# One weight job looked ahead instead of two, and h loaded straight into the place of its low part, in a fused attention and two-MoE kernel

## The chip, the cores and the metric

The kernel runs on one NeuronCore of a Trainium2 chip. The metric is the device time of one execution in microseconds (us). TensorE (PE in the profile) multiplies, VectorE (DVE), ScalarE (ACT) and GpSimd (POOL) do the work between, SyncE (SP) issues nearly all DMAs from one queue, in order. Each engine takes its instructions in program order, so one that waits holds up all that stand behind it on that engine.

## What is computed

```python
def _attn_ref(x, state):                       # x 8x8x512x64, state 8x8x32x64
    a = softmax(scale * x @ state.T)           # each token over the 32 states
    xread = a @ state
    a2 = softmax(scale * state @ x.T)          # each state over the 512 tokens
    sread = a2 @ x
    return concatenate([xread, sread], axis=2)

def _moe_ref(x, w_gate, w_val, w_out):         # 512 -> 1536 -> 512
    gate = 1.0 / (1.0 + np.exp(-(x @ w_gate)))
    return gate * (x @ w_val) @ w_out

def _moe2_ref(x, w_in, w_out):                 # 512 -> 2048 -> 512
    h = x @ w_in
    g = np.where(h >= 1, h, np.where(h <= -1, 0.0, (h + 1) ** 2 / 4))
    return g @ w_out
```

The attention's output, as 4352 tokens of 512 (8 batches of 512 tokens and 32 states), goes through the first MoE and then the second. All of it is float32. The kernel gets float32 accuracy by splitting every operand into a high part (rounded to the matmul's fp32r type) and a low part (what is left), and adding three products: high by high, high by low, low by high.

## The kernel before

The batches are handled in two groups of four. The stages that the change touches, in order of time, are the first gated pass (group 0, `gated(0)`), the first output pass (`output1(0)`, with the attention of group 1 worked in between as "items" of `slot1`), the second gated pass (`gated(1)`) and the second output pass (`output1(1)`). Then come the few tokens of the states, and the second MoE, which takes the second half of the time.

**A gated pass** makes h, the product of gate and value, without forming the attention's output. For every block of 64 rows of the weights a "pair" of matmuls on TensorE (L483) folds the state into them; ACT copies the result as the high half of a tile M (L488), and DVE takes the low half (L494). Then `quads` (L510) multiply M with the attention weights. Twenty-four steps i alternate gate (even, into PSUM set 0) and value (odd, into set 1). The sums of an even step are read by ACT's sigmoid (L551), those of an odd step by a product on DVE (L554); both are emitted in the next step, after its first three heads. A pair of step i goes to the other set: the pair of an odd step needs the set-0 sums of the step before to be read by the sigmoid.

**Weights** come as jobs through the class `Weights`. A job is loaded (tile `wraw`, three buffers, L146), ACT makes two words from it (`parts`: tiles `ca`, three buffers, L155, and `cy`, two buffers, L156), DVE joins them (`join`, L162 and L166), ACT takes the high part (`high`, L181, into the tile `w`), DVE or POOL the low part (`low`, L187). The tile `ca` is held from `parts` to `low`. One `slot` does one step of each, in the order `high`, `join`, `low`, `parts`, `load`; the list `mid` holds joined jobs that wait for `high`. `high` leaves a job alone while its kind is in `closed`; the kind "wo" (the weights of the first output pass) is closed until that pass begins, the kind "m1" (those of the second gated pass) until late in it. In the second gated pass there are two `w` tiles, and each is also stored to `ws_dram` (L466) before its buffer is used again.

**An output pass** multiplies h with w_out. It runs over 24 units (four batches b, six units m2 of 256 rows of h), each of four parts with six matmuls (L624 to L626; the first unit is taken in another order, L606). Before each part, `slot` works items or weight jobs. At unit i the kernel issues the load of unit i + 2 (`load_h`, tile `hraw`, two buffers, L584) and, in part 1, the split of unit i + 1 (`split_h`): ACT makes the high part `oh_hi` (L591), DVE the low part `oh_lo` (L593), two buffers each. After the sixth unit of a batch its sums, two PSUM tiles, are copied into tiles `ev1` by ACT (L632) and by DVE (L634) and stored (L635). In the first pass there is one `ev1` buffer, in the second two. The batches alternate between the PSUM sets; items use the set that the current batch leaves free, which is the set whose sums were just copied out.

Of the kernel before, what the change touches and what calls it, by code (L numbers as in the profile page):

```python
# [25 lines left out]
def attention_moe_moe_kernel(  # L26
# [104 lines left out]
    class Weights:  # L131
# [6 lines left out]
        def __init__(self):  # L138
            self.todo, self.loaded, self.first, self.mid, self.second = [], [], [], [], []

        def load(self, most=9):
            while self.todo and len(self.loaded) + len(self.first) < min(most, CB[0]):
                src, dst = self.todo.pop(0)
                r = conv.tile([128, 1024], U32, tag="wraw", name="wraw", bufs=CB[0])
                for o, i in src(r):
                    nc.sync.dma_start(out=o, in_=i.bitcast(U32))  # L146
                self.loaded.append((r, dst))
# [42 lines left out]

        def slot(self, low=None):
            self.high()
            if len(self.mid) < 2:
                self.join()
            self.low(low)
            if not self.first:
                self.parts()
            self.load()
            flush()
# [377 lines left out]
        return lambda r: [(r, w_out[128 * i : 128 * i + 128])], dst  # L577

    hr_t, h_t, acc_t = {}, {}, {}
    ev_bufs = 1  # L580

    def load_h(b, m2):
        t = hr.tile([128, 2, 512], F32, tag="hraw", name="hraw", bufs=2)
        nc.sync.dma_start(out=t, in_=h_dram[b // 4][:, 2 * m2 : 2 * m2 + 2, b % 4])  # L584
        hr_t[b, m2] = t

    def split_h(b, m2):
        t = hr_t.pop((b, m2))
        hi = hp_.tile([128, 2, 512], F32R, tag="oh_hi", name="oh_hi", bufs=2)
        lo = hp_.tile([128, 2, 512], F32R, tag="oh_lo", name="oh_lo", bufs=2)  # L590
        nc.scalar.activation(out=hi, in_=t, func=AF.Copy)  # L591
        h_t[1, b, m2] = (hi, lo)
        return lambda: nc.vector.tensor_tensor(  # L593
            out=lo, in0=t, in1=f32(hi), op=ALU.subtract
        )

    def out1_first(b, hi, lo, part):
# [16 lines left out]
    def out1(b, m, hi, lo, n, os):  # L614
# [11 lines left out]
            nc.tensor.matmul(out=ps, lhsT=wl[:, c], rhs=hi, start=False, stop=last)  # L626
        if m == NM1 - 1 and os[-1] == 3:
            for i in range(2):
                ev = hp_.tile([128, 2, 512], F32, tag="ev1", name="ev1", bufs=ev_bufs)
                evv = ev[:, :, :n]  # L630
                if i == 0:
                    nc.scalar.activation(out=evv, in_=acc[i][:, :, :n], func=AF.Copy)  # L632
                else:
                    nc.vector.tensor_copy(evv, acc[i][:, :, :n])  # L634
                nc.sync.dma_start(out=y_dram[b][:, 2 * i : 2 * i + 2], in_=evv)  # L635

    def output1(bg, slot):
# [5 lines left out]
        for i, (b, m2) in enumerate(us):  # L643
# [1 line left out]
                load_h(*us[i + 2])  # L645
            hi, lo = h_t.pop((1, b, m2))
            for part in range(4):
                low = split_h(*us[i + 1]) if part == 1 and i + 1 < len(us) else None
                slot(4 * i + part, 1 - b % 2)
                if low:  # L650
                    low()
                if i == 0:
                    if part < 3:
                        out1_first(b, hi, lo, part)
                    continue
                e = part // 2
                os = (0, 1) if part % 2 == 0 else (2, 3)
                out1(b, 2 * m2 + e, hi[:, e], lo[:, e], S, os)
# [373 lines left out]
    for w in PRE:  # L1032
# [45 lines left out]
    sgp = pool("sgp", side="right", stack=st_a)  # L1078
    hp_ = pool("hp", stack=st_h)
    weights.todo += [job_wo(k) for k in range(NM1)]  # L1080
    gated(
        0,
        q_ps,
        {14: lambda: load_h(0, 0), 18: lambda: load_h(0, 1), 23: lambda: split_h(0, 0)()},
    )


# [88 lines left out]


    closed.remove("wo")
    for hp in range(2):
        weights.high()  # L1180
        weights.low()
# [30 lines left out]

    hp_, ev_bufs = pool("hp1", side="right", stack=st_wo), 2
    wsp = pool("wsp", side="right", stack=st_wo)
    st_pa = ExitStack()
    pa = pool("pa", stack=st_pa)
# [131 lines left out]
```

## Time and profile before

| what | value |
|---|---|
| median of 3 runs | 1514.85 us (1513.44 to 1517.57) |
| the profiled execution: its own time | 1514.42 us |
| its span, first to last instruction | 1512.5 us |
| PE busy | 1452.5 us (96%) |
| DVE busy, ACT busy | 908.3 us (60%), 629.1 us (42%) |
| mean granted TensorE clock | 0.984 of full speed |
| first output pass, about 206 to 419 us | PE waits in it below |
| second gated pass, about 419 to 606 us | PE waits in it below |
| second output pass, about 606 to 737 us | PE never idle |

PE is busy nearly all the time, so the time can only fall where PE is idle or where it runs at the lower of its clock levels (0.50 in the rows), and it rises where a new wait reaches PE. In rows of the timeline the first number is the start in us from the span's start, the second the duration, and the bracket at the end tells how long the engine sat idle before the instruction and what ended that.

### The profile page before, as it was taken

The numbers are of one execution on the slowest core, as the hardware profiler recorded it, in microseconds if no ns is written. First come the engines' busy times: TensorE is split into PE (matmuls) and PEld (weight loads), VectorE is DVE, ScalarE is ACT, GpSimd is POOL, SyncE is SP. The second block draws the span as 40 slices with busy tenths as digits, with TensorE's granted clock in tenths as the row PEclk, the third lists the DMA queues.
The fourth block names the chain that finished last, engine by engine and source line by source line (L and its number), as shares of the span: only waits on it lengthen the run. The fifth ranks groups of instructions, "written<-read, shape, count | busy, mean of one in ns | idle before, by whom it ended". The sixth has DMA issues, their size and how long they took to land.

```text
span 1512.5 us, 28809 instructions
## 1 busy us (share of the span) xinstructions
PE 1452.5 (96%) x12176; PEld 1244.4 (82%) x12176; DVE 908.3 (60%) x1201; ACT 629.1 (42%) x896; POOL 32.0 (2%) x25
## 2 busy tenths in 40 slices
PE   7999989899969999999999999999999999999997
PEld 6677767787747778888998888888889899999997
DVE  6666656544346552444227675566655987777785
ACT  6655546343354542343126442233323544444342
POOL 2200003000000000000000000000000000000000
PEclk9999999999979999999999999999999999999999
DMA  6244557543545653675347873553334544344432
GB/s 214 79 156 169 194 177 250 170 158 108 186 168 196 225 209 113 210 248 196 140 171 247 269 247 139 195 182 136 128 140 143 179 140 134 125 134 140 140 126 84
DMA packets 143697, 255.63 MB, mean 169 GB/s; under 512 B 15056, under 2 KB 85712, under 8 KB 143568
## 3 DMA queue, kind: packets, MB, share of 16 engines
q1 hardware_dynamic: 143304, 253.54, 49.2%
q8 instruction: 95, 1.56, 0.4%
q10 hardware_dynamic: 264, 0.26, 0.1%
q14 instruction: 34, 0.28, 0.1%
HBM read 156.24 MB, written 97.52 MB: 168 GB/s over the span
## 4 chain that ended last, share of the span: by engine, by line
PE 84%; DVE 6%; ACT 3%; DMA 3%; issue 3%; SPq 1%; DVEq 0%; ACTq 0%
PE ps L510 15%; PE ps L216 9%; PE ps L218 9%; PE ps L217 9%; PE o L837 7%; PE o L839 7%; PE o L838 7%; PE ps L624 5%; PE ps L626 5%; PE ps L625 5%; PE ps L483 3%; DVE cy L162 1%; PE ps L293 1%; DVE hc L885 1%; ACT cy L156 1%
## 5 line engine op out<-in xcount | busy, mean ns | idle before, releaser
L510 PE MATMUL ps<-at_hi,M 32*128 32x512 f32 x3072 | 265.4, 404 | 9.2 <-DVE M L494 6.4
L839 PE MATMUL o<-w,hc 128*128 128x256 f32 x952 | 267.6, 281 | 3.3 <-DVE hc L885 3.3
L837 PE MATMUL o<-w,hc 128*128 128x256 f32 x952 | 267.4, 281 | 1.9 <-DVE sg L829 1.6
L838 PE MATMUL o<-w,hc 128*128 128x256 f32 x952 | 267.1, 281 | 0.0
L216 PE MATMUL ps<-y_hi,wi 128*128 128x512 f32 (+1 forms) x576 | 217.4, 377 | 0.0
L218 PE MATMUL ps<-y_hi,wi 128*128 128x512 f32 (+1 forms) x576 | 217.3, 377 | 0.0
L217 PE MATMUL ps<-y_lo,wi 128*128 128x512 f32 (+1 forms) x576 | 217.3, 377 | 0.0
L510 PEld LDWEIGHTS ps<-at_hi,M 32*128 32x128 f32 x3072 | 155.6, 187 | 56.7 <-issue 15.6
L839 PEld LDWEIGHTS o<-w,hc 128*128 128x128 f32 x952 | 180.7, 190 | 4.4 <-DVE hc L885 4.4
L837 PEld LDWEIGHTS o<-w,hc 128*128 128x128 f32 x952 | 181.5, 191 | 2.4 <-issue 2.2
L838 PEld LDWEIGHTS o<-w,hc 128*128 128x128 f32 x952 | 180.6, 190 | 0.0
L828 ACT ACTIVATE sg<-sg,half 128x1024 f32<-128x1024 f32 (+1 forms) x72 | 79.6, 1106 | 217.1 <-DVE sg L825 213.3
L510 PE MATMUL ps<-at_lo,M 32*128 32x512 f32 x1536 | 160.9, 398 | 0.0
L624 PE MATMUL ps<-oh_hi,wo 128*128 128x512 f32 x368 | 150.1, 408 | 3.0 <-ACT oh_hi L591 3.0
L625 PE MATMUL ps<-oh_lo,wo 128*128 128x512 f32 x368 | 145.7, 396 | 0.6 <-DVE oh_lo L593 0.5
L626 PE MATMUL ps<-oh_hi,wo 128*128 128x512 f32 x368 | 145.4, 395 | 0.0
L829 DVE TENSOR_TENSOR sg<-sg,ps 128x1024 f32<-128x1024 f32 (+1 forms) x72 | 83.7, 1162 | 86.7 <-ACT sg L828 86.7
L494 DVE TENSOR_TENSOR M<-ps,M 128x1024 fp32r<-128x1024 f32 x48 | 58.8, 1224 | 117.8 <-ACT M L488 117.8
L216 PEld LDWEIGHTS ps<-y_hi,wi 128*128 128x128 f32 x576 | 108.4, 188 | 20.2 <-ACT ev L632 0.2
L217 PEld LDWEIGHTS ps<-y_lo,wi 128*128 128x128 f32 x576 | 108.4, 188 | 20.0
L218 PEld LDWEIGHTS ps<-y_hi,wi 128*128 128x128 f32 x576 | 108.4, 188 | 19.8
L881 ACT ACTIVATE hc<-hc 128x512 fp32r<-128x512 f32 (+1 forms) x108 | 64.9, 602 | 124.1 <-DMA hc<-hd_dram 111.3
(120 smaller groups left out, 2132.7 us busy)
## 6 DMA issues: line engine op xcount, KB each, us to landing
hd_dram<-sg SPq DMA_DIRECT2D x64, 512.0 KB, 2.8
h_dram<-sg SPq DMA_DIRECT2D x48, 512.0 KB, 4.3
hraw<-h_dram SPq DMA_DIRECT2D x48, 512.0 KB, 4.8
hc<-hd_dram SPq DMA_DIRECT2D x96, 256.0 KB, 4.0
wraw<-in_moe_w_out_dram SPq DMA_DIRECT2D x28, 512.0 KB, 4.1
wraw<-in_moe_w_gate_dram SPq DMA_DIRECT2D x48, 256.0 KB, 2.9
wraw<-in_moe_w_val_dram SPq DMA_DIRECT2D x48, 256.0 KB, 3.3
ws_dram<-w SPq DMA_DIRECT2D x24, 512.0 KB, 5.1
```

What stands on the lines that cost most here:

```text
L216: nc.tensor.matmul(out=ps, lhsT=wh, rhs=vh, start=(i == 0), stop=False)
L217: nc.tensor.matmul(out=ps, lhsT=wh, rhs=vl, start=False, stop=False)
L218: nc.tensor.matmul(out=ps, lhsT=wl, rhs=vh, start=False, stop=(i == n - 1))
L510: nc.tensor.matmul(out=ps[r // 2][:, r % 2], lhsT=M[o, l, e, c], rhs=a[o, e], start=(h == 0 and j == 0), stop=(h == H - 1 and j == 2),)
L624: nc.tensor.matmul(out=ps, lhsT=wh[:, c], rhs=hi, start=first, stop=False)
L625: nc.tensor.matmul(out=ps, lhsT=wh[:, c], rhs=lo, start=False, stop=False)
L626: nc.tensor.matmul(out=ps, lhsT=wl[:, c], rhs=hi, start=False, stop=last)
L828: nc.scalar.activation(out=sg, in_=sg, func=AF.Square, bias=half, scale=0.5)
L829: nc.vector.tensor_tensor(out=sg, in0=sg, in1=ps, op=ALU.max)
L837: nc.tensor.matmul(out=ps, lhsT=wh, rhs=vh, start=start and i == 0, stop=False)
L838: nc.tensor.matmul(out=ps, lhsT=wh, rhs=vl, start=False, stop=False)
L839: nc.tensor.matmul(out=ps, lhsT=wl, rhs=vh, start=False, stop=last)
```

## The change

- `Weights` gets a number `ahead`, 1 at first: a slot joins a job only while fewer than `ahead` jobs stand in `mid` (2 before). It is set to 2 at step 18 of the first gated pass and back to 1 at the start of the first output pass.
- `load_h` writes h to the place where its low part will stand, three tiles `oh_lo0` to `oh_lo2` in turn, and the low part is taken in place. The tiles `hraw` are gone; two of the three new tiles take their room, so the total is the same and leaves room for a second `ev1` buffer in the first output pass.
- The split of unit 1 is emitted in part 0 of unit 0, ahead of that part's slot.

```diff
+            self.ahead = 1
...
         def slot(self, low=None):
             self.high()
-            if len(self.mid) < 2:
+            if len(self.mid) < self.ahead:
                 self.join()
...
     def load_h(b, m2):
-        t = hr.tile([128, 2, 512], F32, tag="hraw", name="hraw", bufs=2)
-        nc.sync.dma_start(out=t, in_=h_dram[b // 4][:, 2 * m2 : 2 * m2 + 2, b % 4])
+
+        k = m2 % 3
+        t = (hp_ if k == 2 else hr).tile(
+            [128, 2, 512], F32R, tag=f"oh_lo{k}", name=f"oh_lo{k}", bufs=1
+        )
+        nc.sync.dma_start(out=f32(t), in_=h_dram[b // 4][:, 2 * m2 : 2 * m2 + 2, b % 4])
         hr_t[b, m2] = t
...
     def split_h(b, m2):
-        t = hr_t.pop((b, m2))
+        lo = hr_t.pop((b, m2))
         hi = hp_.tile([128, 2, 512], F32R, tag="oh_hi", name="oh_hi", bufs=2)
-        lo = hp_.tile([128, 2, 512], F32R, tag="oh_lo", name="oh_lo", bufs=2)
-        nc.scalar.activation(out=hi, in_=t, func=AF.Copy)
+        nc.scalar.activation(out=hi, in_=f32(lo), func=AF.Copy)
         h_t[1, b, m2] = (hi, lo)
         return lambda: nc.vector.tensor_tensor(
-            out=lo, in0=t, in1=f32(hi), op=ALU.subtract
+            out=lo, in0=f32(lo), in1=f32(hi), op=ALU.subtract
         )
...
-                ev = hp_.tile([128, 2, 512], F32, tag="ev1", name="ev1", bufs=ev_bufs)
+                ev = hp_.tile([128, 2, 512], F32, tag="ev1", name="ev1", bufs=2)
...
-                low = split_h(*us[i + 1]) if part == 1 and i + 1 < len(us) else None
+                early = part == (1 if i else 0)
+                low = split_h(*us[i + 1]) if early and i + 1 < len(us) else None
...
+    def last_jobs():
+        weights.ahead = 2
+        load_h(0, 1)
+
     gated(
         0,
         q_ps,
-        {14: lambda: load_h(0, 0), 18: lambda: load_h(0, 1), 23: lambda: split_h(0, 0)()},
+        {14: lambda: load_h(0, 0), 18: last_jobs, 23: lambda: split_h(0, 0)()},
     )
...
     closed.remove("wo")
+    weights.ahead = 1
```

TensorE's and POOL's instructions stand in the same order as before, and through the first gated pass so do all others. Three places show what moves. The first is ACT at the start of the first output pass, before and then after (`e2` are the exponentials of the state's attention, `oh_hi` the high part of unit 1):

```order
L156 ACTIVATE cy_3527<-wraw_2870 128x512
L369 ACT_TABLE_LOAD
L369 ACTIVATE e2_283,r2_3504<-ps1_3492,m2_3501 128x512 x2
L369 ACTIVATE e2_355,r2_3521<-ps1_3509,m2_3518 128x512 x2
L155 ACTIVATE ca_3555<-wraw_2994 128x512
L156 ACTIVATE cy_3556<-wraw_2994 128x512
L591 ACTIVATE oh_hi_3571<-hraw_2874 128x1024
L181 ACTIVATE wo0_3_3583<-ca_3526 128x512
```

```order
L158 ACTIVATE cy_3526<-wraw_2870 128x512
L595 ACTIVATE oh_hi_3544<-oh_lo1_2874 128x1024
L371 ACT_TABLE_LOAD
L371 ACTIVATE e2_283,r2_3503<-ps1_3491,m2_3500 128x512 x2
L371 ACTIVATE e2_355,r2_3520<-ps1_3508,m2_3517 128x512 x2
L157 ACTIVATE ca_3556<-wraw_2994 128x512
L158 ACTIVATE cy_3557<-wraw_2994 128x512
L183 ACTIVATE wo0_3_3581<-ca_3525 128x512
```

The high part of unit 1 moves ahead of the table load and the four exponentials. On DVE the low part of unit 1 keeps its place, behind the sums of those exponentials.

The second place is ACT at the start of the second gated pass, with the semaphores that each instruction waits for, before and then after:

```order
L488 ACTIVATE M_5287<-ps0_5280 128x1024 [waits DVE_49,PE_49]
L181 ACTIVATE w_5290<-ca_3894 128x512 [waits DMAHW3_49]
L155 ACTIVATE ca_5295<-wraw_5044 128x512 [waits DMAHW2_49,DMAHW1_49,DVE_49]
L156 ACTIVATE cy_5296<-wraw_5044 128x512
L488 ACTIVATE M_5310<-ps1_5303 128x1024 [waits PE_49]
L181 ACTIVATE w_5313<-ca_5040 128x512 [waits DMAHW0_49]
L155 ACTIVATE ca_5318<-wraw_5125 128x512 [waits DMAHW7_49,DMAHW6_49,DVE_49]
```

```order
L490 ACTIVATE M_5254<-ps0_5247 128x1024 [waits DVE_49,PE_49]
L183 ACTIVATE w_5257<-ca_5010 128x512 [waits DMAHW1_49]
L157 ACTIVATE ca_5262<-wraw_5014 128x512 [waits DMAHW7_49,DMAHW0_49]
L158 ACTIVATE cy_5263<-wraw_5014 128x512
L490 ACTIVATE M_5277<-ps1_5270 128x1024 [waits PE_49]
L183 ACTIVATE w_5280<-ca_5090 128x512 [waits DMAHW6_49,DVE_49]
L157 ACTIVATE ca_5285<-wraw_5094 128x512 [waits DMAHW5_49,DMAHW4_49,DVE_49]
```

The kinds of instructions stay; the first `ca` no longer waits for DVE, and `w` now does. One job fewer is joined ahead during the first output pass (two DVE and two ACT instructions of it are gone there and come back near the end of the gated pass).

The third is SP in the first output pass, the loads of h (units 2 to 4) between the loads of w_out, before and then after:

```order
L584 DMA hraw_3543<-h_dram_0_99 128x2x512 [waits DMAHW2_49,Activation_49]
L146 DMA wraw_3559<-in_moe_w_out_dram 128x1024 [waits DMAHW3_49,DVE_49,Activation_49]
L146 DMA wraw_3593<-in_moe_w_out_dram 128x1024 [waits DMAHW4_49,DVE_49,Activation_49]
L584 DMA hraw_3603<-h_dram_0_99 128x2x512 [waits DMAHW5_49,Activation_49]
L146 DMA wraw_3615<-in_moe_w_out_dram 128x1024 [waits DMAHW6_49,DVE_49]
L146 DMA wraw_3643<-in_moe_w_out_dram 128x1024 [waits DMAHW3_49,DMAHW7_49,DVE_49,Activation_49]
L584 DMA hraw_3657<-h_dram_0_99 128x2x512 [waits DMAHW2_49,DMAHW0_49,Activation_49]
```

```order
L589 DMA oh_lo2_3542<-h_dram_0_99 128x2x512 [waits DMAHW2_49]
L148 DMA wraw_3560<-in_moe_w_out_dram 128x1024 [waits DMAHW3_49,DVE_49,Activation_49]
L148 DMA wraw_3591<-in_moe_w_out_dram 128x1024 [waits DMAHW4_49,DVE_49]
L589 DMA oh_lo0_3601<-h_dram_0_99 128x2x512 [waits DMAHW5_49,PE_49]
L148 DMA wraw_3613<-in_moe_w_out_dram 128x1024 [waits DMAHW6_49,DVE_49]
L148 DMA wraw_3640<-in_moe_w_out_dram 128x1024 [waits DMAHW3_49,DMAHW7_49,DVE_49,Activation_49]
L589 DMA oh_lo1_3654<-h_dram_0_99 128x2x512 [waits DMAHW0_49,PE_49]
```

The loads stand in the same places, but from unit 3 on they wait for PE: the tile that they fill was read by the matmuls of the unit three before.

## Rows read from the trace of the kernel before

**Rows 1.** Stretches: length, busy us of PE, PEld, DVE, ACT, POOL, clock, DMA.
```profile
425.00:610.00 185.00, 171.40 (x2447) 128.64 (x2440) 95.05 (x110) 82.96 (x109) 0.00 (x0) 0.94 0.50 184
...
423.81:450.74 26.93, 18.01 (x149) 11.12 (x149) 14.31 (x19) 14.19 (x21) 0.00 (x0) 0.69 0.60 209
450.74:456.90 6.16, 6.16 (x50) 4.53 (x54) 3.11 (x4) 2.63 (x4) 0.00 (x0) 0.51 0.10 16
...
610.00:740.00 130.00, 130.00 (x587) 108.06 (x587) 51.39 (x57) 43.76 (x57) 0.00 (x0) 1.00 0.59 196
```

**Rows 2.** Waits, 418 to 610 us: who waited for whom, total us, times, longest.
```profile
ACT ca L155 <- DVE w L187: 52.9, 19, 4.3
...
PE ps L483 <- ACT sg L551: 7.1, 8, 2.4
```

**Rows 3.** Timeline where the first batch of the first output pass ends.
```profile
264.31 8.71 SPq L635 DMA_DIRECT2D y_dram<-ev  x2
271.44 1.22 DVE L634 COPY ev<-ps 128x1024 f32<-128x1024 f32 x1 [7.67 <-DMA y_dram<-ev]
272.72 1.97 PE L386 MATMUL ps<-ident,e 128*128 128x128 f32 x8 [4.05 <-DVE ev L634]
...
277.38 1.10 PE L278 MATMUL ps<-ident,xa 128*128 128x128 f32 x8 [0.68 <-ACT e L317]
```

**Rows 4.** Timeline of the start of the first output pass.
```profile
219.84 0.17 DVE L377 TENSOR_SCALAR r<-r 128x2 f32<-128x2 f32 x1 [0.97 <-ACT e L369]
220.83 1.04 ACT L591 ACTIVATE oh_hi<-hraw 128x1024 fp32r<-128x1024 f32 x1
221.90 1.22 DVE L593 TENSOR_TENSOR oh_lo<-hraw,oh_hi 128x1024 fp32r<-128x1024 f32 x1 [0.38 <-ACT oh_hi L591]
221.92 0.79 PE L624 MATMUL ps<-oh_hi,wo 128*128 128x512 f32 x1 [2.96 <-ACT oh_hi L591]
223.18 0.80 PE L625 MATMUL ps<-oh_lo,wo 128*128 128x512 f32 x1 [0.46 <-DVE oh_lo L593]
```

**Rows 5.** Timeline of the start of the second gated pass.
```profile
419.85 1.02 ACT L488 ACTIVATE M<-ps 128x1024 fp32r<-128x1024 f32 x1 [1.27 <-PE ps L483]
...
421.40 1.23 DVE L634 COPY ev<-ps 128x1024 f32<-128x1024 f32 x1 [6.72 <-ACT w L181]
422.54 1.22 DVE L494 TENSOR_TENSOR M<-ps,M 128x1024 fp32r<-128x1024 f32 x1
...
423.81 0.79 PE L510 MATMUL ps<-at_hi,M 32*128 32x512 f32 x2 [2.38 <-DVE M L494]
...
425.00 0.69 DVE L187 TENSOR_TENSOR w<-ca,w 128x512 fp32r<-128x512 f32 x1
...
425.72 0.67 ACT L155 ACTIVATE ca<-wraw 128x512 f32<-128x512 f32 x1 [4.33 <-DVE w L187]
...
426.84 1.00 ACT L488 ACTIVATE M<-ps 128x1024 fp32r<-128x1024 f32 x1
...
443.92 1.23 DVE L494 TENSOR_TENSOR M<-ps,M 128x1024 fp32r<-128x1024 f32 x1 [2.19 <-ACT M L488]
...
447.11 0.68 ACT L155 ACTIVATE ca<-wraw 128x512 f32<-128x512 f32 x1 [2.70 <-DVE w L187]
...
450.74 1.65 PE L483 MATMUL ps<-w,sd 64*128 64x512 f32 x6 [2.44 <-ACT sg L551]
...
467.57 0.97 PE L483 MATMUL ps<-w,sd 64*128 64x512 f32 x6 [0.68 <-ACT sg L551]
```

**Rows 6.** DMAs issued 420 to 460 us: times issued, KB each, median us to landing.
```profile
ws_dram<-w SPq DMA_DIRECT2D x6, 512.0 KB, 3.7
```

**Rows 7.** Loads of h over both output passes: time to landing, 48 loads.
```profile
DMA to landing us min/median/max: 3.5/4.8/8.1
```

**Rows 8.** Timeline: TensorE's start and end of the second output pass.
```profile
606.05 0.50 PE L606 MATMUL ps<-oh_hi,wo 128*128 128x512 f32 x1
...
736.80 0.31 PE L216 MATMUL ps<-xs_hi,ws 128*128 128x256 f32 x1
```

## What the change will do to the time, forecast before it was run

> **What bounds the kernel now.** I read the page first: PE is busy 96% of the span, so a change that touches no matmul can only win where PE is idle or runs at its lower clock. Then the stretches, stage by stage [rows 1]. The second output pass shows PE busy 130.00 us of 130.00 at clock 1.00: nothing to win, only something to lose. The second gated pass shows 171.40 of 185.00 at a mean clock of 0.94. Its start is the weak place: of the 26.93 us from 423.81 to 450.74 PE works 18.01, much of it at the lower level, and the 6.16 us after that run at 0.51, the lower level of the two (1.2 GHz against 2.4). Then the waits of that pass [rows 2]: PE waits 7.1 us, eight times, for ACT's sigmoid, and ACT itself stands 52.9 us, 19 times, with the instruction that fills `ca` until DVE has taken the low part of a weight. Last the timeline at the three places where PE stands: the end of the first batch of the first output pass [rows 3], that pass's start [rows 4], the start of the second gated pass [rows 5].
>
> **One depth instead of two.** The 19 waits have a reason that can be counted in the code. `ca` has three buffers, each held from `parts` to `low`. Two jobs in `mid` and one between `high` and `low` fill them, so the `ca` of a slot needs the `low` of the same slot. That closes a ring over two engines, which [rows 5] shows: M's low part on DVE at 422.54, two joining instructions, `w` at 425.00 to 425.69 (3.15 us from 422.54), `ca` on ACT at 425.72, `cy`, and only then the next M, 1.12 us later at 426.84, 1.00 long, for which DVE waits. 3.15 + 0.03 + 1.12 + 1.00 + 0.04 = 5.34 us. The low part of M at 443.92 is four rounds later: 21.38 / 4 = 5.35. With one job in `mid` the third buffer was freed a slot earlier, and ACT fills it at once. What is late next: DVE's own four instructions, 3.15 us; ACT's own four, about 2.7 (M 1.00, `ca` and `cy` 1.12, `w` estimated at 0.6 from `ca`'s 0.67); and a new pair of waits, since `w` must now see the join of the slot before (over by then, as DVE joins ahead of its `low`), and each of the two `w` buffers must be stored before it is used again. Such a round, `low` 0.69, store landing 3.7 [rows 6], `w` about 0.6, is 5.0 us for two slots, though `w` stands behind M on ACT and can be pushed back by it. Bounds for a slot: 3.15 and, if the store always comes last behind M and the joins, about 4.3. I take 3.3, near DVE's, because the store's round is shorter than two of DVE's. Four rounds then take 13.2 us instead of 21.4: **8.2 us** less (4.2 to 8.8).
>
> From the last of these M to the pair at 450.74 lies a second part: ACT stands 2.70 us before `ca` at 447.11, then comes `cy`, the table load and the sigmoid that PE waits for. That wait goes too; the store may take some back. **2.0 us** (0.7 to 2.7). A check from PE's side: with 10.2 us gone, 16.7 of 26.93 remain for 18.01 us of matmuls, most of them at the lower level. So if PE stayed as slow as it is, it would be the bound, and 8.9 would be the gain; the shorter pauses should let some of it run at full speed. Afterwards 6.16 us run at 0.51, which costs 3.0; I take **1.0** of that back (0 to 3.0), as the pauses ahead are shorter but not gone.
>
> Later in the pass the same wait delays the sigmoid in each odd step: the first of the eight waits is the 2.44 at 450.74, the other seven sum to 4.7, each like the 0.68 at 467.57 [rows 2, 5]. ACT's wait before `ca` there is some 2.7 us (52.9 / 19), so the sigmoid can start when its sums are ready. **4.7 us** (3.5 to 4.7). The join that is no longer made ahead adds four instructions, 0.7 us each, near the end of the pass, where DVE and ACT are half busy (95.05 and 82.96 of 185.00): nothing. In the first gated pass the limit stops no job that moves, nothing.
>
> **Two `ev1` buffers in the first output pass.** DVE's copy of the first batch's second half stood 7.67 us until 271.44 for the store of the first half to leave the one buffer [rows 3]. Without that it runs 263.77 to 264.99; PE, free at 268.67, then finds its PSUM tile empty and saves 4.05. The eight transposes behind the pause took 1.97 against 1.10 for eight at full speed, and some matmuls behind them were slow too; together I add 1.5. **5.6 us** (4.05 to 6). Next late is the 0.68 before L278, which stays. The same happens to the last batch: the copy at 421.40 is put down to ACT's `w`, but it is the store issued when the first half was copied. M's low part can follow ACT's M, which ends at 420.87, instead of starting at 422.54: **1.65 us** [rows 5], and the matmuls at 423.81 come that much earlier. At the other two batches PE showed no such wait: nothing.
>
> **The early split of unit 1.** PE stood 2.96 us for the high part of unit 1 [rows 4]. That part now comes ahead of the exponentials, so the first matmul can go. But the second matmul wants the low part, and on DVE that stands behind the sums of those exponentials (the wait at 219.84), which the moved instruction pushes back by its 1.04, less the overlap of neighbours, 0.95. DVE had 0.38 to spare before the low part, so it comes 0.57 later, and PE with it. I expect no gain but a **loss of 0.55 us** (a gain of at most 0.5, a loss of 1.0); PE's wait is renamed.
>
> **Loads of h into the low part's place.** The load of unit i + 2 used to wait for the split of unit i, now for PE to finish unit i - 1, which is the start of unit i. A unit takes (736.80 - 606.05) / 24 = 5.45 us [rows 8]. From there to the start of unit i + 2 are 10.9 us; less the high part 1.04, the low part 1.22 and some 0.4 of hand-overs, a load may take 8.2. Loads took 3.5 to 8.1, 4.8 in the middle [rows 7]. So the cover is just enough, by the unit of matmuls between; if it fails, PE pays what is over 8.2. Behind the waiting load on SP stand the weights, the x tiles and the stores of the unit; the stores wait for PE at the end of a batch anyway, and the weights of this stage are wanted a slot or more later. **Loss 0.3 us** (0 to 3), from 0 because most loads are far from the edge.
>
> **Sum.** Against the profiled execution's own 1514.42 (span 1512.5): 8.2 + 2.0 + 1.0 + 4.7 + 5.6 + 1.65 - 0.55 - 0.3 = 22.3, so 1492.1. The median of the runs is 0.43 above the profiled one: 1492.5. The ends of the terms together give 1489 to 1501, but not all fall on one side.
>
> **Rivals.** (1) *The store's round takes the ring's place.* For it: DMA is busy 0.60 in the start of the gated pass [rows 1], and a faster chain asks more of it per us. Slots of 4.3: the four rounds give 4.2, the tail 0.7, the clock nothing: 22.3 - 4.0 - 1.3 - 1.0 = 16.0, 1498.5. (2) *The wait for DVE is only a name.* If DVE's and PE's order hold the slot at 5.34 whatever ACT does, only the `ev1` terms stay: 5.6 + 1.65 - 0.85 = 6.4, 1508. Against it: after each of these waits ACT goes on without a pause into the M that DVE waits for. (3) *Slower: loads come late.* The place is every unit from the third on, 22 in each output pass; the price is what a landing takes beyond 8.2 us. To eat the forecast it needs 0.5 us in each of 44 units, to end 4.5 us slower 0.61, so landings of 8.8 throughout; at 9.0 it would be 1492.5 + 35 = 1528. Against it: the longest of 48 took 8.1 [rows 7]. The Trainium skill (Trainium Kernel Development and Optimization, Best Practices) asks to double-buffer so that DMA overlaps compute, and a change that shortens both look-aheads goes against that; by that rule it would end here. The 52.9 us of ACT [rows 2] speak against the rule: there the second job in front is what makes an engine stand. (4) *The gains and costs cancel, or the change does not do what it says.* The order of the instructions shows the `ca` without DVE's wait, so this is small.
>
> **How the numbers follow.** The forecast, 1487 to 1496.5, has a chance of 0.68; (1), 1496.5 to 1502, 0.17; (2), 1503 to 1510, 0.07; (3) 0.04; (4) 0.04. The forecast and (1) hold 0.85, so the range is 1487 to 1502. About 0.3%, 4.5 us, is what a measurement of this kernel can tell from no change: faster by more 0.92, within it 0.04, slower 0.04.
>
> **What would show it.** ACT's wait for DVE before `ca` should be nearly gone in the second gated pass, the low parts of M 3.2 to 3.6 us apart at its start, and the 7.1 us of PE's waits for the sigmoid below 2. DVE's copy should follow ACT's within 3 us at the end of the first batch. PE should still stand 2.5 to 4.5 us at the start of the first output pass, now for the low part. In the second output pass PE should stay busy throughout. I am wrong if the M's stay 5.3 apart (2), if `w` waits for its store (1), or if PE waits for `oh_hi` in the output passes (3).

## The result, and the profile after

The changed kernel takes 1491.55 us (median of 4 runs, 1490.81 to 1496.89); the kernel before took 1515.78 beside it (4 runs, 1513.44 to 1517.57). The ratio is 0.985, with a 95% interval of 0.982 to 0.988: 1.5%, or 23 us between the means (24 between the medians). The forecast was 1492.5, from 1487 to 1502. The profiled execution took 1490.97 us, its span 1489.2, at a mean clock of 0.994 (0.984 before).

The first view shows the stretches of the changed kernel, cut where PE starts the same instructions as in the kernel before. Columns: stretch, length, busy us (and instructions) of PE, PEld, DVE, ACT and POOL, then granted clock, DMA share, GB/s.

```profile
211.92:268.87 56.95, 48.63 (x289) 38.68 (x288) 38.35 (x49) 36.68 (x59) 15.43 (x9) 0.94 0.83 265
268.87:272.16 3.29, 2.45 (x16) 1.82 (x14) 3.29 (x3) 2.03 (x3) 0.00 (x0) 1.00 0.56 221
272.16:413.29 141.13, 139.11 (x1140) 113.26 (x1140) 61.77 (x86) 53.61 (x70) 0.00 (x0) 1.00 0.46 146
413.29:416.96 3.67, 2.48 (x19) 1.24 (x17) 2.51 (x3) 2.40 (x5) 0.00 (x0) 1.00 0.68 276
416.96:434.58 17.62, 12.29 (x149) 7.55 (x150) 14.21 (x19) 13.41 (x20) 0.00 (x0) 1.00 0.78 260
434.58:582.17 147.59, 147.59 (x2286) 115.66 (x2286) 79.30 (x90) 68.22 (x90) 0.00 (x0) 1.00 0.55 199
582.17:712.98 130.81, 130.81 (x580) 107.96 (x577) 53.86 (x59) 44.76 (x57) 0.00 (x0) 1.00 0.59 193
```

The names of these seven stretches are used below: **a** from the first matmul of the first output pass to the transposes behind its first batch (268.87; 272.72 before, [rows 3]); **b** to the next transposes; **c** to the last matmul of the pass; **d** to the first quads with a low part of M (416.96; 423.81 before); **e** to the pair behind the first sigmoid (434.58; 450.74 before, [rows 5]); **f** to the second output pass; **g** that pass. Each row of the table is worked out from the starts of those instructions in one profiled execution, in us.

| kernel | a | b | c | d | e | f | g |
|---|---|---|---|---|---|---|---|
| before | 59.82 | 4.66 | 141.14 | 5.30 | 26.92 | 155.31 | 130.75 |
| changed | 56.95 | 3.29 | 141.13 | 3.67 | 17.62 | 147.59 | 130.81 |
| saved | 2.87 | 1.37 | 0.01 | 1.63 | 9.30 | 7.72 | -0.06 |

They sum to 22.8 us. The rest of the 23.3 us between the two spans lies where nothing was changed: the first output pass began at 211.92 instead of 212.90, and what follows the second one took 776.22 instead of 775.70. The kernel before in stretch f, of which 4.68 us are PE's pauses:

```profile
450.74:606.05 155.31, 150.63 (x2287) 115.36 (x2287) 78.10 (x88) 68.76 (x89) 0.00 (x0) 0.98 0.49 181
```

Then the second gated pass of the changed kernel. First its waits, 396 to 590 us (who waited for whom, us in total, times, longest), which answer [rows 2]:

```profile
ACT w L183 <- DMA ws_dram<-w: 2.8, 1, 2.8
...
PE ps L485 <- ACT w L183: 1.8, 1, 1.8
ACT w L183 <- DVE M L496: 1.3, 1, 1.3
...
PE ps L485 <- ACT sg L553: 0.5, 1, 0.5
```

ACT's wait before `ca`, 52.9 us in 19 pieces before, is gone altogether, and of PE's 7.1 us of waits for the sigmoid 0.5 are left. New is one wait of ACT for the store of `w`. The timeline of DVE and ACT at the start of the pass, for [rows 5]:

```profile
415.67 1.23 DVE L496 TENSOR_TENSOR M<-ps,M 128x1024 fp32r<-128x1024 f32 x1 [0.73 <-ACT M L490]
...
418.74 1.22 DVE L496 TENSOR_TENSOR M<-ps,M 128x1024 fp32r<-128x1024 f32 x1
...
421.81 1.22 DVE L496 TENSOR_TENSOR M<-ps,M 128x1024 fp32r<-128x1024 f32 x1
...
423.77 0.63 ACT L183 ACTIVATE w<-ca 128x512 fp32r<-128x512 f32 x1 [2.77 <-DMA ws_dram<-w]
...
426.46 1.23 DVE L496 TENSOR_TENSOR M<-ps,M 128x1024 fp32r<-128x1024 f32 x1 [1.34 <-ACT M L490]
...
427.73 0.63 ACT L183 ACTIVATE w<-ca 128x512 fp32r<-128x512 f32 x1 [1.30 <-DVE M L496]
...
430.42 1.22 DVE L496 TENSOR_TENSOR M<-ps,M 128x1024 fp32r<-128x1024 f32 x1 [0.80 <-ACT M L490]
```

The low parts of M, 5.35 us apart before, come 3.07, 3.07, 4.65 and 3.96 apart. 3.07 is DVE with no pause between its four instructions. The third gap is long because ACT could not write the next `w` until the store of the one two slots earlier had landed. The fourth follows a second wait of ACT before `w`, which is put down to DVE here. In the second profile of the changed kernel (first experiment below) the two waits are there again, with the names the other way round:

```profile
423.18 0.63 ACT L183 ACTIVATE w<-ca 128x512 fp32r<-128x512 f32 x1 [2.64 <-DVE cy L164]
...
427.45 0.63 ACT L183 ACTIVATE w<-ca 128x512 fp32r<-128x512 f32 x1 [1.62 <-DMA ws_dram<-w]
```

So both are taken for waits for the store; the run with a third `w` buffer tests that.

The end of the first batch of the first output pass of the changed kernel, DVE, SP and PE, for [rows 3] (each engine in its own order of time):

```profile
264.10 1.22 DVE L638 COPY ev<-ps 128x1024 f32<-128x1024 f32 x1
...
262.87 2.82 SPq L639 DMA_DIRECT2D y_dram<-ev  x2
...
268.87 1.03 PE L388 MATMUL ps<-ident,e 128*128 128x128 f32 x8
```

DVE's copy no longer waits (7.67 us before) and PE's transposes follow without a pause, at full speed (1.03 against 1.97). The start of that pass, for [rows 4]:

```profile
214.63 1.05 ACT L595 ACTIVATE oh_hi<-oh_lo 128x1024 fp32r<-128x1024 f32 x1
...
219.82 0.17 DVE L379 TENSOR_SCALAR r<-r 128x2 f32<-128x2 f32 x1 [0.97 <-ACT e L371]
...
221.42 1.22 DVE L597 TENSOR_TENSOR oh_lo<-oh_lo,oh_hi 128x1024 fp32r<-128x1024 f32 x1
...
222.69 0.79 PE L629 MATMUL ps<-oh_lo,wo 128*128 128x512 f32 x1 [4.49 <-DVE oh_lo L597]
```

PE still stands, now for the low part, in one piece of 4.49 us where it was 2.96 and 0.46 before: DVE takes the sums of the exponentials and a join first, although the high part has been there since 215.7. Counted from the pass's start, this second matmul of unit 1 comes at 10.77 us instead of 10.28.

### The profile page after: what moved, and what is told of

Its sections match the earlier page's. It is cut to its first block, busy times and chain, and to the rows that moved or that the text cites. A ratio compares the mean times of both kernels' runs of the same rounds, so it can differ in the third digit from the quotient of the medians.

```text
span 1489.2 us, 28842 instructions
## 1 busy us (share of the span) xinstructions
PE 1441.2 (97%) x12176; PEld 1240.0 (83%) x12176; DVE 908.5 (61%) x1201; ACT 628.6 (42%) x896; POOL 31.8 (2%) x25
## 4 chain that ended last, share of the span: by engine, by line
PE 88%; DVE 5%; DMA 3%; ACT 2%; issue 1%; SPq 1%; DVEq 0%; ACTq 0%
PE ps L512 18%; PE ps L218 9%; PE ps L220 9%; PE ps L219 9%; PE o L844 7%; PE o L842 7%; PE o L843 7%; PE ps L628 6%; PE ps L629 5%; PE ps L630 5%; PE ps L485 3%; PE ps L295 1%; PE ps L280 1%; DVE cy L164 1%; DMA hc<-hd_dram 1%
## 5 line engine op out<-in xcount | busy, mean ns | idle before, releaser
L512 PE MATMUL ps<-at_hi,M 32*128 32x512 f32 x3072 | 260.9, 397 | 6.7 <-DVE M L496 3.9
```

Of the source, the lines that this page charges most:

```text
L512: nc.tensor.matmul(out=ps[r // 2][:, r % 2], lhsT=M[o, l, e, c], rhs=a[o, e], start=(h == 0 and j == 0), stop=(h == H - 1 and j == 2),)
```

## The experiments

Single executions of the changed kernel spread over 6 us (1490.81 to 1496.89), and medians of one kernel differ by about 2 us from one group of runs to the next (changed: 1491.55 and 1489.89; before: 1513.55 to 1515.78). Part of this lies outside the changed stages: in the first 60 us, which no experiment touches, one execution was granted 0.94 of the clock (the changed kernel) and another 0.83 (the one with four buffers for raw weights), the first output pass began between 211.2 and 215.6, and what follows stretch g took 773.3 to 779.9.

```profile
0.00:60.00 60.00, 45.83 (x392) 38.75 (x394) 40.53 (x48) 41.40 (x52) 16.37 (x16) 0.94 0.50 159
```
```profile
0.00:60.00 60.00, 48.40 (x350) 41.33 (x354) 37.40 (x44) 38.18 (x48) 16.35 (x16) 0.83 0.47 150
```

The stretches repeat far better, so each experiment is read by its stretch first. c is 141.13 to 141.19 and g 130.75 to 130.95 in every kernel here but one, the one with two places for h.

| kernel | median us | a | b | d | e | f |
|---|---|---|---|---|---|---|
| changed | 1491.55 | 56.95 | 3.29 | 3.67 | 17.62 | 147.59 |
| changed, again | 1489.89 | 57.16 | 3.30 | 3.68 | 17.77 | 147.36 |
| before + one job ahead | 1494.33 | 59.16 | 4.66 | 5.30 | 16.98 | 147.36 |
| changed, two jobs ahead | 1507.44 | 57.17 | 3.30 | 3.68 | 26.90 | 154.14 |
| changed, one `ev1` | 1495.36 | 58.78 | 4.66 | 5.30 | 16.49 | 147.36 |
| two ahead, four `ca`, three `sg` | 1505.82 | 57.23 | 3.29 | 3.67 | 18.90 | 161.14 |
| two ahead, four `ca` | 1495.29 | 57.08 | 3.30 | 3.67 | 18.81 | 147.60 |
| late split | 1491.93 | 57.06 | 3.29 | 3.67 | 18.00 | 147.61 |
| low part first | 1492.82 | 57.69 | 3.29 | 3.67 | 17.67 | 147.60 |
| low part first, sums last | 1490.52 | 55.56 | 3.30 | 3.67 | 17.59 | 147.36 |
| three `w` | 1491.49 | 57.09 | 3.30 | 3.67 | 16.04 | 147.60 |
| three `w`, four raw | 1492.18 | 57.36 | 3.30 | 3.68 | 15.13 | 147.60 |

**The changed kernel again**, as the measure for the last runs.

> The changed kernel once more, as the measure for the runs beside it: 1491.6 us, within 3.

1489.89 us, ratio to before 0.983 (0.981 to 0.985). The stretches agree with the first profile within 0.25 us.

**One job ahead, alone.** The kernel before with `ahead` only:

```diff
...
-            if len(self.mid) < 2:
+            if len(self.mid) < self.ahead:
...
```

> The kernel before with one edit: jobs joined ahead are one instead of two from the first output pass on; the staging tile of h, the single ev1 buffer and the place of the split stay as before. Ring theory (three ca buffers and two jobs ahead tie ACT's ca to DVE's low part): the second gated pass gives what its two stretches gave in the changed kernel, 9.3 us from the first quads to the first sigmoid's pair and 7.7 us from there to the second output pass, so 17 us less than before, about 1498.5; ACT's wait for DVE in front of ca is gone; the 4.05 us pause of PE at the end of the first batch and DVE's wait before the copy of the last batch stay. Rival (the wait for DVE is only a name, the gain came from the ev1 buffers and the clock): within 3 us of before.

1494.33 us, ratio 0.988 (0.986 to 0.990): e falls by 9.9 and f by 8.0, a, b and d keep the single `ev1`. This edit alone carries 18 of the 23 us. The rival that the wait is only a name (1508 in the prediction) is out. The low parts of M at the start of the pass:

```profile
420.40 1.21 DVE L495 TENSOR_TENSOR M<-ps,M 128x1024 fp32r<-128x1024 f32 x1
...
433.47 1.22 DVE L495 TENSOR_TENSOR M<-ps,M 128x1024 fp32r<-128x1024 f32 x1
```

Four rounds take 13.07 us here, against 21.4 before and 14.75 in the changed kernel, which starts the pass earlier.

**Two jobs ahead in the changed kernel.**

```diff
-            self.ahead = 1
+            self.ahead = 2
...
-    weights.ahead = 1
+    weights.ahead = 2
```

> The changed kernel with two jobs ahead throughout. Ring theory: the second gated pass loses 17 us again, about 1508.5, with ACT's wait for DVE in front of ca back at some 50 us and the low parts of M about 5.3 us apart at the start; the ev1 gains (5.4 and 1.6 us) stay. Rival (the wait is only a name): within 3 us of the changed kernel.

1507.44 us, ratio to before 0.996 (0.994 to 0.997). ACT's waits in the second gated pass are back as they were:

```profile
ACT ca L157 <- DVE w L189: 55.5, 20, 4.2
```

e is 26.90, f 154.14: 9.3 and 6.6 us lost again, 15.8 of the 17 that were expected. The low parts of M are 5.34 us apart.

**Four `ca` buffers with two jobs ahead.** This separates the ring (three buffers for two jobs) from the look-ahead as such. The room for the fourth was first taken from `sg`:

```diff
-                a = conv.tile([128, 512], U32, tag="ca", name="ca", bufs=CB[1])
+                a = self.ca_tile()
...
-                        sg_t[t] = sgp.tile([128, 2, 512], F32, tag="sg", name="sg", bufs=4)
+                        sg_t[t] = sgp.tile([128, 2, 512], F32, tag="sg", name="sg", bufs=sg_bufs)
```

> The changed kernel with two jobs ahead throughout, but a fourth ca buffer in the second gated pass (paid for with three sg buffers instead of four there). Ring theory: what made ACT wait was the third buffer, not the second job; with four buffers the time is that of the changed kernel within 2 us, about 1492, and ACT does not wait for DVE in front of ca. Rival (two jobs ahead cost because DVE joins a later job ahead of the low part that PE waits for, or because more is in flight): the loss stays whatever the buffers, 1505 to 1509.

1505.82 us, ratio 0.995 (0.993 to 0.996): by the total, the rival had won. The stretches say otherwise: e is 18.90, not far from the 17.62 with one job, but f is 161.14. The waits, 396 to 590 us:

```profile
ACT sg L559 <- DMA h_dram<-sg: 21.7, 6, 4.4
...
ACT ca L163 <- DVE w L195: 6.9, 2, 4.2
```

The wait before `ca` is down to its first two pieces, before the fourth buffer comes in; what cost the time is the new wait of the sigmoid for a store, since `sg` has three buffers. So the run had changed two things at once. It was repeated with `sg` at four and the fourth `ca` in a place of h that is not yet in use then:

> As the run with a fourth ca buffer and two jobs ahead, but the fourth buffer is the place of a tile of h that is not in use yet (until step 13 of the second gated pass), and sg keeps its four buffers. If the third ca buffer was the cause and the three sg buffers were what cost time in that run (ACT's sigmoid waited 21.7 us there for its store): the stretch from the first sigmoid's pair to the second output pass falls from 161.1 to 148 us, the whole to 1491 to 1494. If two jobs ahead cost by themselves: 1503 or more.

1495.29 us, ratio 0.987 (0.986 to 0.989); f is 147.60, e 18.81. So in f two jobs ahead cost nothing when `ca` has a buffer for each job that holds one. The ring is shown: not the look-ahead, the missing buffer. The 1.2 us more in e are not in the four rounds, which take 14.59 us here although the first is still 5.33; they come behind them, where ACT waits for the store of `w` again:

```profile
432.61 0.63 ACT L190 ACTIVATE w<-oh_lo 128x512 fp32r<-128x512 f32 x1 [1.37 <-DMA ws_dram<-w]
```

Most of the rest of the distance between the two profiled executions lies behind stretch g (779.9 us, the longest of all), where the edit changes nothing; why is not shown.

**One `ev1` buffer in the changed kernel.**

```diff
-                ev = hp_.tile([128, 2, 512], F32, tag="ev1", name="ev1", bufs=2)
+                ev = hp_.tile([128, 2, 512], F32, tag="ev1", name="ev1", bufs=ev_bufs)
```

> The changed kernel with one ev1 buffer in the first output pass. If the two buffers are worth what the trace shows (4.05 us of pause and 1.4 us of slow matmuls at the end of the first batch, 1.6 us at the start of the second gated pass), 7.1 us more than the changed kernel, about 1498.6. Rival (the shorter ring would have hidden the late start, since the pass's start is bound by the two engines' chain and not by PE): only the 5.4 us of the first batch, 1497. Second rival (PE's pause is shifted to the next wait): under 2 us.

1495.36 us, ratio 0.988 (0.986 to 0.990): 3.8 us more than the changed kernel, not 7.1. a gives 1.83 of it, b 1.37, d 1.63, and e takes 1.13 back. It is also the run with one job ahead alone, plus the loads into the low part's place and the early split: 1495.36 against 1494.33 beside it, so these two by themselves gain nothing that can be seen. What the loads bring is the room for the second `ev1`. Three more things are to be seen. DVE's copy and PE behind it, in this run:

```profile
269.93 1.23 DVE L639 COPY ev<-ps 128x1024 f32<-128x1024 f32 x1 [5.01 <-DMA y_dram<-ev]
...
271.21 1.09 PE L388 MATMUL ps<-ident,e 128*128 128x128 f32 x8 [1.39 <-DVE ev L639]
```

and in the run with one job ahead alone, which has one `ev1` too:

```profile
269.31 1.23 DVE L635 COPY ev<-ps 128x1024 f32<-128x1024 f32 x1 [6.02 <-DMA y_dram<-ev]
...
270.58 1.97 PE L387 MATMUL ps<-ident,e 128*128 128x128 f32 x8 [2.40 <-DVE ev L635]
```

The wait for the same store was 7.67, 6.02 and 5.01 us in three executions and PE's pause 4.05, 2.40 and 1.39. The profile that the prediction read was at the long end: there the store was issued 1.81 us after ACT's copy had ended (0.02 and 0.03 in the other two); by the profile SP's queue stood 1.1 us of it for a load of x. From the issue to DVE's copy it took 7.13, 7.28 and 6.26 us.

Second, b is 4.66 us with one `ev1` whether PE runs it slowly (clock 0.66 before, 0.65 with one job ahead alone) or at full speed, as here:

```profile
271.21:275.87 4.66, 2.50 (x15) 1.88 (x15) 4.59 (x6) 2.02 (x3) 0.00 (x0) 1.00 0.69 225
```

So the 1.37 us of b are not the clock's: DVE, busy for 4.59 us of it, comes late to the work behind its copy, and PE's next transposes start 5.93 to 5.94 us after that copy in all three executions.

Third, the 1.63 us by which the second gated pass starts earlier with two buffers (d) come back for the most part in e: ACT's waits that are put down to the store of `w` ahead of the sigmoid are 0.68 and 0.89 us in this run; the two before `w` in the changed kernel are 2.77 and 1.30 (next experiment).

**A third `w` buffer** up to step 9 of the second gated pass, in a place of h:

```diff
...
-            t = wp.tile([128, 2, 512], F32R, tag="w", name="w", bufs=w_bufs)
+            if spare_w and i % 3 == 2:
+                t = hr.tile([128, 2, 512], F32R, tag="oh_lo1", name="oh_lo1", bufs=1)
+            else:
+                t = wp.tile([128, 2, 512], F32R, tag="w", name="w", bufs=w_bufs)
...
```

> The changed kernel with a third buffer for w up to step 9 of the second gated pass (the place of a tile of h not in use yet). If the round over the store of w is what holds the start of that pass now (ACT stood 2.77 and 1.30 us there), the low parts of M come 3.07 apart throughout, the first sigmoid 2.5 us earlier: the stretch from the first quads to the first sigmoid's pair takes 15.1 instead of 17.6 us, the whole 2.5 us less than the changed kernel. Rival (DMA is the bound there, its share is 0.71: the weights come late instead): no gain, ACT waits for wraw.

1491.49 us, ratio 0.985 (0.983 to 0.987); e is 16.04, 1.6 us shorter instead of 2.5. The wait for the store is gone from the rounds: three of them are now 3.07 long; the fourth is 4.13, for a wait of ACT that the profile puts down to DVE:

```profile
427.91 0.69 ACT L157 ACTIVATE ca<-wraw 128x512 f32<-128x512 f32 x1 [1.78 <-DVE cy L164]
```

This was tried with **a fourth buffer for the raw weights** as well:

```diff
...
+                if self.more and self.n % 4 == 0:
+                    r = hr.tile([128, 2, 512], F32R, tag="oh_lo0", name="oh_lo0", bufs=1)
...
```

> As the run with three w buffers, with a fourth buffer for the raw weights as well, in another place of h that is not in use yet, up to step 9. If the wait of 1.78 us that ACT had there behind the store round was for the raw weights, the low parts of M come 3.07 apart throughout and the stretch from the first quads to the first sigmoid's pair takes 15.1 us, against 16.0 there and 17.6 in the changed kernel: 2.5 us less than the changed kernel in all. If the DMA engines are the bound (share 0.81 there): 16 us or more, as with three w buffers alone.

e is 15.13, as reckoned, with all low parts 3.06 or 3.07 apart:

```profile
421.07:436.21 15.14, 12.24 (x149) 7.66 (x150) 13.94 (x19) 13.48 (x20) 0.00 (x0) 1.00 0.87 311
```

So that wait went with a buffer for the loads: it was for the raw weights, not for DVE. DVE is busy for 13.94 of the 15.14 us, so it is the likely bound now, though no run speeds it up to show it. In the whole, 1492.18 us (0.985, 0.982 to 0.987) can't be told from the changed kernel; the profiled execution lost 3.7 us before the first output pass, where nothing differs.

**The split of unit 1.** First back in its old place:

```diff
-                early = part == (1 if i else 0)
+                early = part == 1
```

> The changed kernel with the split of unit 1 in its old place, at part 1 of unit 0, behind the exponentials. By the prediction the early split costs 0.55 us, so this is 0.5 us faster than the changed kernel (0 to 1.0): PE waits 3.0 us for the high part and 0.5 for the low part instead of 4.5 for the low part alone. Rival (the early high part lets PE begin and so gains): up to 0.5 us slower.

1491.93 us (0.986, 0.984 to 0.987); a is 57.06 against 56.95 and 57.16. The second matmul of unit 1 comes 0.45 us earlier, counted from the pass's start (10.32 against 10.77), as reckoned, but at the end of the stretch nothing is left of it. The waits of PE in stretch a:

```profile
PE ps L628 <- ACT oh_hi L595: 3.0, 1, 3.0
PE ps L280 <- DVE sd L129: 3.0, 1, 3.0
PE ps L629 <- DVE oh_lo L597: 1.7, 3, 0.8
```

Then with the low part ahead of the sums on DVE:

```diff
+                if low and not i:
+                    low()
+                    low = None
                 slot(4 * i + part, 1 - b % 2)
```

> The changed kernel with the low part of unit 1 issued on DVE right behind its high part, ahead of the sums of the exponentials and of the joins. If DVE's order alone makes PE stand 4.49 us there, the second matmul starts at about 218.0 instead of 222.7; next late is the low part of the fourth row block of w_out on POOL, done at 223.8, which PE then wants at about 221.5: a gain of 2.2 us, 1 more if the clock stays up. Rival (PE's pause only moves to that row block because POOL is pushed back too): no gain.

1492.82 us (0.986, 0.983 to 0.988). The second matmul starts at once, and PE's pauses apart from the 3.0 for `sd` fall from 5.3 to 3.1 us. The fourth row block of w_out is next late, on ACT (1.38 us) and, as expected, on POOL (1.07). But a is 57.69, 0.5 to 0.7 longer, because the granted clock in it was 0.88 instead of 0.94: behind the pauses of 1.38 and 1.07 us PE runs at the lower level from 225.80 to 234.98, 0.63 us a matmul instead of 0.40.

```profile
213.71:271.40 57.69, 51.66 (x290) 40.41 (x289) 38.82 (x49) 36.71 (x59) 15.54 (x9) 0.88 0.82 265
```

Last with the sums behind DVE's joins too:

```diff
...
-        nc.vector.tensor_scalar(out=r2, in0=r2, scalar1=1e-9, scalar2=None, op0=ALU.add)
-        nc.vector.reciprocal(out=r2, in_=r2)
+
+        def sums():
+            nc.vector.tensor_scalar(out=r2, in0=r2, scalar1=1e-9, scalar2=None, op0=ALU.add)
+            nc.vector.reciprocal(out=r2, in_=r2)
+
+        late.append(sums)
...
```

> The changed kernel with the low part of unit 1 right behind its high part, as in the run before of that name, and the sums of the exponentials behind DVE's joins as well, so that the row block of w_out on POOL is not pushed back: the three pauses of that run (1.38, 1.07, 0.47 us) should go, and of the 4.49 us of the changed kernel nothing be left. If pauses set the time: 2 to 4.5 us less than the changed kernel between the pass's start and the end of its first batch (56.95 us there). If TensorE's clock takes back what the pauses give (in the run before the pauses were 2.2 us less, but 0.79 of the clock was granted in the first 20 us against 0.91, and the stretch was 0.7 longer): within 1 us of it.

```profile
213.03:268.59 55.56, 46.77 (x289) 36.13 (x288) 37.91 (x47) 36.62 (x59) 15.17 (x9) 1.00 0.81 266
```

PE is idle for 8.8 us of this stretch (6.0 in the run before it, 8.3 in the changed kernel), now in nine pieces, and yet a is the shortest of all, since PE ran at the upper level throughout. The 4.49 us did not vanish as expected, they were spread over smaller pauses; the gain of 1.4 to 1.6 us is the clock's (PE busy 46.77 us for the same matmuls, against 48.63 in the changed kernel). The total, 1490.52 (0.984, 0.982 to 0.985), is again the changed kernel's.

**Two places for h instead of three**, which takes one unit of cover from each load:

```diff
-        k = m2 % 3
-        t = (hp_ if k == 2 else hr).tile(
+        k = m2 % 2
+        t = hr.tile(
```

> The changed kernel with two places for h and its low part instead of three, so that a load waits for PE to finish the unit before, not the one before that. By the reckoning of the prediction a place then goes round in one unit of matmuls (5.45 us in the second output pass), the landing (4.4 us in the middle), the high part 1.04, the low part 1.22 and 0.4 of hand-overs, 12.5 us for two units, against 10.9 of PE: 0.8 us lost in each of 22 units, 18 us in the second output pass (9 to 30, more if the clock falls), and about nothing in the first, where a unit takes 8.4 us with the other work between. About 1510. Rival (the loads had far more cover than reckoned, or wait for something else): under 3 us. Second rival (a landing is paid in full by each unit): 1.7 us in each, 37 us, 1529.

1524.26 us, slower than before: ratio 1.006 (1.005 to 1.008), 34 us more than the changed kernel beside it. g is 141.10, 10.3 longer; the first output pass loses 22 (a 66.8, c 153.2), where about nothing was expected. PE's waits in the first pass:

```profile
PE ps L414 <- DMA xr<-in_x_dram: 6.4, 2, 5.0
PE ps L629 <- DVE oh_lo L597: 5.3, 2, 4.5
PE ps L280 <- DMA xa<-in_x_dram: 4.5, 1, 4.5
PE ps L628 <- ACT oh_hi L595: 3.0, 1, 3.0
```

Two of the four are tiles of x, not of h. They stand on SP's queue behind a load of h that waits for PE:

```profile
258.42 0.38 SPq L589 DMA_DIRECT2D oh_lo<-h_dram  x1
258.83 0.98 SPq L265 DMA_DIRECT2D xa<-in_x_dram  x2
...
263.13 2.21 PE L280 MATMUL ps<-ident,xa 128*128 128x128 f32 x8 [4.52 <-DMA xa<-in_x_dram]
```

The queue's own waits for PE before a load of h are 147.7 us in 21 pieces in this pass, against 60.3 in 13 in the changed kernel. In the second pass a place goes round in 12.1 us (loads issued at 646.83 and 658.93), where 12.5 had been reckoned, and its units take 5.88 on average, 0.43 more than PE needs, where 0.8 had been worked out.

## Why the prediction was right, point by point

The mechanism of the largest part, the ring over `ca`, was right and is shown by three runs. That the sum came out to 0.5 us (22.3 against 22.8 in the changed stages) was luck: the clock gave 2.0 us more than its term, the ring and the tail 0.9 less than theirs, and the first batch with the split and the loads 0.6 less.

- **The ring and the tail** (8.2 + 2.0): e gave 9.30. The mechanism stands: one job alone brings it, two jobs take it back, a fourth `ca` undoes it at two jobs. Alone the sizes hold too: with the single `ev1` the four rounds took 13.07 us (13.2 in the prediction) and e gave 9.94. What failed is that this term and the last batch's were added as if they did not meet. In the changed kernel the first M comes 1.63 us earlier, and from the third round on the store of `w` binds: the rounds took 3.07, 3.07, 4.65 and 3.96 where I took 3.3 for each, which gives 6.6 of the 8.2, and the tail 2.7 instead of 2.0. So rival (1), and the sign that I had named for it, came true in part. With a buffer more for the store's round and for the raw weights e is 15.13, 11.8 less than before.
- **The clock after 450.74** (1.0, up to 3.0): f gave 7.72, of which 4.68 was PE's idle time in it and the other 3.0 the clock, all of it. What failed is the size, not the reason given for it: the pauses ahead were shorter but not gone, as predicted (5.3 us of e instead of 8.9, the longest 2.52 us at 431.70), and yet after 434.58 PE runs at the upper level without a break. Nor did PE's speed in e matter: in the second profile of the changed kernel the clock there was 0.81 and e 17.77, against 1.00 and 17.62.
- **The seven later sigmoid waits** (4.7): 4.68.
- **Two `ev1` buffers, first batch** (5.6): mis-sized. a and b together gave 4.24 with the split and the loads in them; the experiment on the buffer alone gave 3.2. The step that failed is to take the 4.05 for the whole gain of a: that is one execution's pause, behind a store that stood in SP's queue (4.05, 2.40 and 1.39 in three), and the changed kernel lost 1.2 us of it again before it came to the same place: 0.45 by the time of the transposes that wait for `sd` and 0.73 behind them, where PE fell to the lower level (last section). The 1.5 for slow matmuls came out in b (1.37) for another reason than the one given: with one `ev1`, b is 4.66 at the upper level too.
- **Two `ev1` buffers, last batch** (1.65): d gave 1.63, as worked out, but e lost 1.1 of it again to the store of `w`, the same us that the ring's term is short. A start that comes earlier helps only as far as the next thing is ready.
- **The early split** (-0.55): PE's wait was renamed and 0.45 late, as worked out, but against the run with the late split nothing of it is left at the end of the stretch.
- **Loads into the low part's place** (-0.3): nothing, c and g are unchanged. The cover is enough; how much of it is spare was not measured, but one unit less costs 34 us. Where I reckoned it with 5.45 us a unit for both passes, the first pass's units take 8.4 (201 us for 24), so its own loads have more cover; what fails there first is SP's queue behind a waiting load, which the prediction named without a price.
- **The ends of the terms**: their bounds add up to 1487.5 and 1504.8, not to the 1489 and 1501 of the prediction.

Of the signs, the gaps between the low parts of M missed the 3.2 to 3.6 us on both sides; the others came out.

The Trainium skill (Trainium Kernel Development and Optimization, Best Practices) asks to double-buffer so that DMA overlaps compute. For the loads of h two places are such a double buffer, and they cost 34 us against three: a place is held through the load, the split and PE's matmuls, and that round (12.1 us) is longer than PE's two units (10.9). For the joined jobs, which are no DMA, a second one in front gained nothing with its own buffer and cost 16 us without.

## What to carry to other kernels

Count, for each tile that a look-ahead holds, from where it is taken to where it is freed: if the items in flight equal the buffers, the producer waits for the consumer of the same step, and a shorter look-ahead or one more buffer opens the ring. A single execution's wait for a store is one draw; price it as a range. Two gains that meet at the same place, here a faster chain and an earlier start of it, are to be priced together: the next bound can take one of them. And where an edit's total comes out as nothing, cut the trace at the same instructions in both kernels before believing it: a second wait may have taken the gain, and the untouched stretches alone differ by several us.

## What the runs showed of the hardware that was not expected

In stretch a PE's granted clock decided more than its pauses did. With 8.3 us idle the clock was 0.94 (56.95 us), with 6.0 idle 0.88 (57.69), with 8.8 idle in nine pieces 1.00 (55.56). In the first two PE fell to the lower level behind a pause at the start of the pass (4.49 us; 1.38 and 1.07 us) and once more behind its wait for `sd` (2.97 and 2.95 us). In the third it stood for `sd` just as long and did not fall. The transposes behind that wait, in the changed kernel and then in the third run:

```profile
253.42 1.97 PE L280 MATMUL ps<-ident,xa 128*128 128x128 f32 x8 [2.97 <-DVE sd L129]
```
```profile
254.05 1.09 PE L280 MATMUL ps<-ident,xa 128*128 128x128 f32 x8 [2.95 <-DVE sd L129]
```

In the kernel before they took 1.09 too, behind 2.95 us. So the length of a pause alone does not tell whether the level falls; what does was not isolated. DVE's wait for one and the same store differed by 2.7 us between three executions: up to 1.8 by when SP's queue came to issue it, and 1.0 by the time from the issue until DVE went on. And the name that a wait carries can be another's: ACT's 1.78 us before `ca`, put down to DVE, went with a buffer for a DMA, and its two waits before `w` changed names between two profiles of one kernel.
